# Strided sparse attention and a multiplicative FFN: the first batch's first q and k loads as eight rows a partition with the head pairs stacked on partition halves, and another order of its scores and tails

## The chip, the cores and the metric

The kernel runs on one core of a Trainium2 chip. The metric is the device time of one execution in microseconds (us), here the median of three runs. A profiled execution gives the trace from which the single durations come.

## What is computed

q, k and v have the shape (8 batches, 8 heads, 576 rows, 64), all fp32. Heads 0 to 3 attend to a causal window of 32 keys ("local"), heads 4 to 7 to earlier keys with the same row number modulo 32 ("strided"). The output of the attention, as 4608 tokens of 512, goes through an FFN:

```python
scores = scale * np.matmul(q, k.transpose(0, 1, 3, 2))
scores = np.where(masks[None], scores, -1000000000.0)   # local for h < 4, strided for the others
attn = np.exp(scores - scores.max(-1, keepdims=True))
attn = attn / (attn.sum(-1, keepdims=True) + 1e-09)
x = np.matmul(attn, v)                                  # then (B, H, S, D) -> (B*S, H*D)
out = ((x @ w1) * (x @ w2)) @ w3 @ w_out                # d_model 512, d_ff 1024
```

## The kernel before, in words

Heads are treated in pairs: p0 and p1 are the local pairs of batch 0, p2 and p3 its strided ones. All matmuls take fp16; the inputs are fp32 in HBM and are cast on the chip. q and k must stand with the head dimension on the partitions (two heads of 64 fill 128), so each is loaded with rows on the partitions, cast, transposed by TensorE (a matmul with an identity) into PSUM, and copied to `qT` and `kT`. The first 512 rows of a head go this way with four consecutive rows on a partition (row 4p+c is chunk c of partition p); the last 64 rows, "the rest", are loaded apart (`load_rest`) and transposed in `ah_R`.

The work of the later batches is threaded between the FFN's matmuls of the tokens before. Batch 0 has nothing to hide behind. Its order is written out by hand in `batch0` (L888): `pe` and, while `head[0]` is set, `pin` keep every instruction in program order on its engine. Its parts are:

- `load_first` (L230) issues the q and k loads of batch 0 on SP's queue, group 0 for p0 and p1, group 1 for p2 and p3: 128 partitions, four heads, four rows of 64 floats, so 1 KB pieces. `cast_first` (L239) casts one pair's part with GpSimd ("p"), ScalarE ("a") or VectorE ("v"). SP's queue then holds the rest, group 1, the four loads of v for the local heads (`load_vL`), and the weights. v for the strided heads (`load_vN`, L277) is issued by ScalarE.
- `T1`, that is `ah_T1` (L442), makes one pair's transposes of q (0) or k (1); `ah_T1c` (L455) copies them out, q of the local pairs on ScalarE, k on VectorE.
- `ah_bias` (L538) writes a mask's bias into a score buffer (pool `psB`, two buffers); `sc`, that is `ah_S0`, adds the scores of half of the query groups, and ScalarE takes the exp into the pair's `ptm` or `nptm`. The second half (`sc(p, 1)`) of the local pairs needs the rest rows.
- `ah_tail` copies 16-row tails of a strided pair's exp to `emb`. `ah_PV` multiplies with v and VectorE normalizes; `ph_T2` transposes the output (pool `psM`, one buffer) and copies it to `xT`, the FFN's input. p1's PV needs the second part of `v16L`: a cast (`stage["l"][1][0]`) and then the copy of a 32-row halo (`stage["l"][1][1]`, `halo`).
- `warm` issues small matmuls whose result nobody reads; they take a buffer of pool `psF` (three buffers), which `T1` and `ah_PV` use too.
- `batch0b` begins the FFN's first matmuls (`aps`) with p0's output and the first part of w1, which GpSimd casts as it lands.

From there the FFN's matmuls run to the end, with the attention of the later batches among them.

Of the kernel before, what the change touches and what calls it, by code (L numbers as in the profile page):

```python
# [8 lines left out]
FP32 = mybir.dt.float32  # L9
# [10 lines left out]
def kernel(  # L20
# [11 lines left out]
    nc = tc.nc  # L32
    B, H, S, D = q.shape
# [3 lines left out]
    P = 128  # L37
# [13 lines left out]
    NM = 512  # L51
# [12 lines left out]
    stgp = ctx.enter_context(tc.tile_pool(name="stgp", bufs=9))  # L64
# [10 lines left out]
    def pe(ins):  # L75
        return tc.keep_in_program_order(ins)
# [6 lines left out]
    def half_rows(u):  # L83
        return slice(64 * u, 64 * u + 64)
# [6 lines left out]
    def copy(eng, out, in_):  # L91
        if eng == "a":
            return pin(nc.scalar.copy(out=out, in_=in_))  # L93
        elif eng == "v":
            return pin(nc.vector.tensor_copy(out=out, in_=in_))  # L95
        return pin(nc.gpsimd.tensor_copy(out=out, in_=in_))  # L96
# [3 lines left out]
    id16 = idw[:, 0:P]  # L100
# [108 lines left out]
    x16 = {}  # L209
# [18 lines left out]
    stage = {}  # L228

    def load_first(grp):  # L230
        for nm, ten in (("q", q), ("k", k)):
            st = stgp.tile([P, 4, 4 * D], FP32, tag="stg", name="st")
            t = qkp.tile([P, 2, 4, 2, D], FP16, tag=f"{nm}{grp}", name="t")
            nc.sync.dma_start(st, ten[0, 4 * grp:4 * grp + 4, 0:NM].rearrange("h (p c) d -> p h (c d)", c=4))
            stage[(nm, grp)] = st
            for i in range(2):
                x16[(nm, 2 * grp + i)] = t[:, i]

    def cast_first(nm, hp, eng):  # L239
        h0 = 2 * (hp % 2)  # L240
        st = stage[(nm, hp // 2)]
        return copy(eng, x16[(nm, hp)], st[:, h0:h0 + 2].rearrange("p h (c d) -> p c h d", c=4))
# [73 lines left out]
    for b in range(B):  # L316
        for hp in range(4):
            s = Pair()
# [123 lines left out]
    def ah_T1(s, i, dst=None):  # L442
        if dst is None:
            dst = psF.tile([P, 2 * NM], FP16, tag="f", name="tps")[:, 0:NM]
        if s.b:
            src = x16[(s.b, "qk"[i], s.hp // 2)]
            h0 = 2 * (s.hp % 2)
        else:
            src, h0 = x16[("qk"[i], s.hp)], 0
        for c in range(4):  # L450
            pe(nc.tensor.transpose(dst[:, c * P:(c + 1) * P],  # L451
                                   src[:, c, h0:h0 + 2].rearrange("p h d -> p (h d)"), id16))
        return dst

    def ah_T1c(s, i, dst, eng=None):  # L455
        t = (qT, kT)[i]
        eng = eng or ("v" if i or s.nat and s.b == 0 else "a")
        if s.local:
            copy(eng, t[:, s.hp, 0:NM].rearrange("x (p c) -> x p c", c=4),
                 dst.rearrange("x (c p) -> x p c", c=4))  # L460
        elif i:
            copy(eng, t[:, s.hp, 0:NM], dst)
        else:
            copy(eng, t[:, s.hp].rearrange("x (c w) -> x c w", w=NW)[:, :, 0:P],
                 dst.rearrange("x (c p) -> x c p", c=4))
# [72 lines left out]
    def ah_bias(s, g, wide=True):  # L538
        kr = s.kr
        cs, lo, hi = ah_group(s, g)  # L540
        if wide:
            sps = psB.tile([P, 2, NB], FP32, tag="big", name="sps")
            outs, full = [sps[:, 0], sps[:, 1]], sps
        else:
            outs, full = [psF.tile([P, NB], FP32, tag="f", name="sph") for _ in range(2)], None
        for h in range(2):
            pe(nc.tensor.matmul(outs[h][0:kr, 0:hi - lo], id16[0:kr, 0:kr], s.bias[:, lo:hi], start=True, stop=False))  # L547
        s.sc = getattr(s, "sc", {})
        s.sc[g] = (outs, full)
# [29 lines left out]
    def ah_PV(s, g):  # L579
        cs, lo, hi = ah_group(s, g)  # L580
        ptm, end = ah_home(s)
        if s.b == 0 or s.local:
            xps = psF.tile([P, NB], FP32, tag="f", name="xpl")[:, 0:390].rearrange("p (h x) -> p h x", h=2)
        else:
            xps = psB.tile([P, 2, NB], FP32, tag="big", name="xps")
        for i, c in enumerate(cs):
            for h in range(2):
                c0 = ah_off(s, g) + h * (hi - lo) + s.q[c] - lo
                m = min(P, end - c0)
                o = xps[0:m, h, i * 65:(i + 1) * 65]  # L590
                tail = s.nat and c == NC
                pe(nc.tensor.matmul(o, ptm[0:s.kr, c0:c0 + m],
                                    s.v[0:s.kr, 2 * (s.hp % 2) + h, c, :], start=True, stop=not tail))
                for e in range(NC if tail else 0):
                    e0 = h * 256 + e * 64
                    pe(nc.tensor.matmul(o, emb[:, s.hp - 2, e0:e0 + P], s.v[:, 2 * (s.hp % 2) + h, e, :],
                                        start=False, stop=e == NC - 1))
        if g == 0:
            s.xqs = att.tile([P, LT, 2, D], FP16, tag="xqs", bufs=2, name="xqs")
        norm(s, xps[0:s.kr, :, 0:len(cs) * 65], cs[0], len(cs))  # L600
# [9 lines left out]
    def ph_T2(s, pool=psM, tag="m", n=0):  # L610
        fill = n
        n = s.n
        ps = pool.tile([P, 1024], FP16, tag=tag, name="t2")

        def tr(t, k, o, j=0):
            pe(nc.tensor.transpose(ps[:, o:o + k], s.xqs[0:k, t].rearrange("p h d -> p (h d)"), idw[0:k, j:j + k]))  # L616

        for t in range(n):
            if s.local:
                tr(t, s.q[t + 1] - s.q[t], s.q[t], 0 if t else P - 32)  # L620
            else:
                tr(t, YW if s.nat and t == NC else P, t * P)
        o = xT[s.hp][:, S * s.b:S * s.b + S]
        warm(ps, fill, 384)
        if s.local:
            copy("a", o, ps[:, 0:S])
        elif s.nat:
            copy("a", o[:, 0:NM].rearrange("x (p c) -> x p c", c=4), ps[:, 0:NM].rearrange("x (c p) -> x p c", c=4))
            copy("v", o[:, NM:S], ps[:, NM:S])
        else:  # L630
            ov = o.rearrange("x (t a c) -> x t a c", a=8, c=4)
            nc.scalar.copy(out=ov[:, :, 0:7], in_=ps[:, 0:NM].rearrange("x (c y) -> x y c", c=4)[:, 1:P - 1]
                           .rearrange("x (t a) c -> x t a c", a=7))
            nc.vector.tensor_copy(out=ov[:, :, 7], in_=ps[:, NM + 28:NM + 28 + YW].rearrange("x (t c) -> x t c", c=4))
# [234 lines left out]
    p0, p1, p2, p3 = pairs[0:4]  # L869
# [6 lines left out]
    def both(s):  # L876
        ah_bias(s, 0)
        ah_bias(s, 1)

    def sc(s, g):  # L880
        ah_S0(s, (g,), False)
# [5 lines left out]

    def batch0():  # L888
        head[0] = True
        cast_first("q", 0, "p")  # L890
        cast_first("q", 1, "a")
        both(p0)
        w = psF.tile([P, 1024], FP16, tag="f", name="warm")
        warm(w, 5)
        t = [T1(p0, 0), T1(p1, 0)]
        for s in (p0, p1):
            ah_T1c(s, 0, t[s.hp])
        load_vN(0)
        warm(w, 3)
        cast_first("k", 0, "v")  # L900
        cast_first("k", 1, "p")
        ah_T1c(p0, 1, ah_T1(p0, 1, psM.tile([P, 1024], FP16, tag="m", name="tps")[:, 0:NM]))
        warm(w, 4)
        ah_T1c(p1, 1, T1(p1, 1))
        copy("p", *stage["r"])
        warm(psF.tile([P, 1024], FP16, tag="f", name="warm"), 8)
        sc(p0, 0)
        ah_R(0)()
        sc(p0, 1)
        cast_first("q", 2, "p")  # L910
        cast_first("q", 3, "p")
        cast_first("k", 2, "v")
        cast_first("k", 3, "p")
        ah_bias(p1, 0)
        sc(p1, 0)
        t = [T1(p2, 0)]
        ah_bias(p1, 1)
        ah_T1c(p2, 0, t[0], "a")
        sc(p1, 1)
        ah_T1c(p2, 1, T1(p2, 1))  # L920
        ah_T1c(p3, 0, T1(p3, 0))
        ah_bias(p2, 0)
        stage["l"][0][0]("p")
        stage["l"][0][1]("v")
        sc(p2, 0)
        ah_T1c(p3, 1, T1(p3, 1))
        ah_bias(p2, 1)
        sc(p2, 1)
        stage["x"]("p")
        stage["l"][1][0]("p")  # L930
        ah_PV(p0, 0)
        ah_bias(p3, 0)
        sc(p3, 0)
        ah_tail(p2, 0)
        ah_tail(p2, 1)
        ah_PV(p0, 1)
        ah_bias(p3, 1)
        sc(p3, 1)
        ah_PV(p2, 0)
        ph_T2(p0)  # L940
        ah_PV(p2, 1)
        ah_tail(p3, 0)
        ah_tail(p3, 1)
        stage["l"][1][1]("a")
        ah_PV(p3, 0)
        ah_PV(p3, 1)
        ph_T2(p2)
        ah_PV(p1, 0)
        ah_PV(p1, 1)
        head[0] = False  # L950
# [29 lines left out]
    for p, s in enumerate(pairs):  # L980
        b, i = divmod(p, 4)
# [77 lines left out]
    for jc in range(KF):  # L1059
        h0, h1 = fold_mm(jc)  # L1060
# [95 lines left out]
```

## Time and profile before

| what | value |
|---|---|
| median of three runs | 267.95 us (267.46 to 268.63) |
| profiled execution: time | 267.3 us |
| profiled execution: span on the core | 265.6 us |
| TensorE's granted clock, mean | 0.998 |
| TensorE matmul busy | 259.7 us, 98% of the span |
| VectorE, ScalarE, GpSimd busy | 60%, 53%, 38% |
| HBM traffic over the span | 38.80 MB read, 9.44 MB written |

The profiled execution's time is what the device took; its span goes from the first to the last recorded instruction of the core. In the profile PE is TensorE's matmuls, PEld its weight loads, DVE VectorE, ACT ScalarE, POOL GpSimd and SP the SyncE, whose queue issues most DMAs. A row of the timeline has the start, the length, the engine, the line, the operation, output<-input, shapes and a count; in brackets the idle time before it and what ended it. A row of the chain of waits has start, length and what. A row of the windows has the stretch, its length, the busy time and count of PE, PEld, DVE, ACT and POOL, the granted clock, the mean busy share of the DMA engines and GB/s. Casts and copies that go through the helper `copy` have the lines L93 (ScalarE), L95 (VectorE) and L96 (GpSimd), whatever they copy.

### The profile page before, as it was taken

How to read it: one execution, taken by the hardware profiler on the slowest of the kernel's cores; microseconds unless marked ns; L12 is line 12 of the kernel's file. 1: busy time of each engine (PE TensorE's matmuls, PEld its weight loads, DVE VectorE, ACT ScalarE, POOL GpSimd, SP SyncE). 2: the span in 40 equal slices, each digit the busy share in tenths (PEclk: the TensorE clock that was granted, in tenths of full speed). 3: DMA queues.
4: the chain of work that ended last, by engine and by line, in shares of the span. 5: the costliest groups of instructions: out<-in, count | busy, mean ns of one | idle time of the engine just before them, and what ended most of it. 6: DMA issues, size and time to landing. Idle time of an engine off the chain costs nothing.

```text
span 265.6 us, 6880 instructions
## 1 busy us (share of the span) xinstructions
PE 259.7 (98%) x2730; PEld 137.7 (52%) x2730; DVE 158.1 (60%) x373; ACT 140.1 (53%) x299; POOL 101.3 (38%) x124
## 2 busy tenths in 40 slices
PE   6999999999999999999999999999999999999995
PEld 5664465555555555555555555555555544444442
DVE  7684443655767777867776777577866752421320
ACT  4674342766666655565556565555557634333322
POOL 7687876866239327602730273038200000000000
PEclk9999999999999999999999999999999999999999
DMA  7999999978388588339823973397330022013004
GB/s 224 350 406 407 416 406 311 243 203 261 129 228 237 194 244 224 111 122 269 241 69 124 283 210 119 118 247 225 109 121 2 0 79 82 0 39 121 0 12 147
DMA packets 61100, 48.68 MB, mean 183 GB/s; under 512 B 31804, under 2 KB 52492, under 8 KB 61068
## 3 DMA queue, kind: packets, MB, share of 16 engines
q1 hardware_dynamic: 56236, 40.38, 49.6%
q10 hardware_dynamic: 4832, 7.87, 8.0%
q8 instruction: 21, 0.34, 0.5%
q14 instruction: 11, 0.09, 0.1%
HBM read 38.80 MB, written 9.44 MB: 182 GB/s over the span
## 4 chain that ended last, share of the span: by engine, by line
PE 91%; ACT 3%; DVE 2%; DMA 2%; issue 0%; SPq 0%; ACTq 0%
PE ops L775 29%; PE aps L723 23%; PE bps L732 22%; PE sps L438 3%; PE pt L350 2%; PE t2a L642 2%; PE sps L401 2%; DMA st<-in_k_dram 2%; PE tps L451 1%; PE sps L535 1%; DVE ptm L413 1%; PE t L616 1%; ACT pte L424 1%; PE sps L547 1%; PE trp L833 1%; ACT nptm L560 1%
## 5 line engine op out<-in xcount | busy, mean ns | idle before, releaser
L723 PE MATMUL aps<-xT,w1h 128*128 128x512 f16 (+1 forms) x288 | 73.2, 376 | 0.2
L732 PE MATMUL bps<-xT,w2h 128*128 128x512 f16 (+1 forms) x288 | 73.1, 376 | 0.0
L735 DVE TENSOR_TENSOR abt<-bps,asb 128x512 f16<-128x512 f32 (+1 forms) x72 | 48.6, 679 | 36.8 <-PE bps L732 34.5
L96 POOL CAST t<-st 128x1024 f16<-128x1024 f32 (+1 forms) x49 | 46.3, 955 | 57.4 <-DMA st<-in_q_dram 44.7
L93 ACT COPY asb<-aps 128x512 f32<-128x512 f32 (+1 forms) x71 | 41.3, 584 | 50.7 <-PE aps L723 44.8
L775 PE MATMUL ops<-w,abt 128*128 128x512 f16 x280 | 67.1, 379 | 0.0
L732 PEld LDWEIGHTS <-w2h 128*128 128x128 f16 x288 | 27.1, 98 | 30.9 <-issue 0.7
L723 PEld LDWEIGHTS <-w1h 128*128 128x128 f16 x288 | 26.9, 98 | 28.8 <-issue 0.3
L775 PEld LDWEIGHTS <-abt 128*128 128x128 f16 x280 | 25.2, 98 | 26.2
L424 ACT ACTIVATE pte<-sps 128x1024 f16<-128x1024 f32 (+1 forms) x24 | 24.4, 1018 | 13.2 <-PE sps L401 12.8
L786 ACT COPY osb<-ops 128x512 f32<-128x512 f32 x35 | 21.0, 599 | 19.5 <-PE ops L775 19.5
L607 DVE TENSOR_TENSOR xqs<-sps,rcp 128x768 f16<-128x768 f32 (+1 forms) x24 | 21.4, 891 | 0.8
L413 DVE TENSOR_TENSOR ptm<-pte,maskE 128x1152 f16<-128x1152 f16 (+2 forms) x16 | 12.3, 770 | 7.3 <-ACT pte L424 6.7
L413 DVE TENSOR_TENSOR ptm<-pte,maskX 126x1152 f16<-126x1152 f16 x12 | 11.5, 958 | 7.6 <-ACT pte L424 7.6
L775 PE MATMUL ops<-woh,w3T 128*128 128x512 f16 x64 | 15.3, 380 | 0.0
L95 DVE COPY kT<-pt 128x512 f16<-128x512 f16 (+4 forms) x28 | 11.4, 416 | 6.4 <-ACT kT L93 4.6
L93 ACT COPY qT<-pt 128x224 f16<-128x224 f16 (+4 forms) x40 | 15.0, 424 | 0.2 <-PE pt L358 0.2
L96 POOL CAST v16L<-st 96x768 f16<-96x768 f32 x16 | 13.2, 824 | 4.7 <-DMA st<-in_v_dram 3.7
L309 POOL CAST v16X<-st 126x1024 f16<-126x1024 f32 x6 | 7.4, 1230 | 19.3 <-DMA st<-in_v_dram 15.2
L438 PEld LDWEIGHTS <-ptm 128*128 128x128 f16 (+1 forms) x264 | 11.0, 98 | 6.0 <-DVE ptm L413 1.4
L95 DVE COPY xT<-t2a 128x384 f16<-128x384 f16 (+1 forms) x22 | 8.5, 388 | 7.3 <-PE t2a L642 6.7
L93 ACT COPY kT<-pt 128x224 f16<-128x224 f16 x24 | 8.5, 353 | 6.7 <-DVE qT L95 6.4
(130 smaller groups left out, 286.0 us busy)
## 6 DMA issues: line engine op xcount, KB each, us to landing
st<-in_q_dram SPq DMA_DIRECT2D x16, 512.0 KB
st<-in_k_dram SPq DMA_DIRECT2D x16, 512.0 KB
st<-in_moe_w_dram SPq DMA_DIRECT2D x16, 512.0 KB
out_dram<-osb ACTq DMA_DIRECT2D x27, 256.0 KB
st<-in_v_dram SPq DMA_DIRECT2D x32, 144.0 KB
st<-in_v_dram SPq DMA_DIRECT2D x24, 112.0 KB
st<-in_moe_w_out_dram SPq DMA_DIRECT2D x4, 512.0 KB
out_dram<-osb SPq DMA_DIRECT2D x8, 256.0 KB
```

What stands on the lines that cost most here:

```text
L93: return pin(nc.scalar.copy(out=out, in_=in_))
L95: return pin(nc.vector.tensor_copy(out=out, in_=in_))
L96: return pin(nc.gpsimd.tensor_copy(out=out, in_=in_))
L413: nc.vector.tensor_mul(o.rearrange("p (a x) -> p a x", x=x), i.rearrange("p (a x) -> p a x", x=x), _ap(s.mask, lo, [[s.mask.ap[0][0], s.kr ...
L424: nc.scalar.activation(out=pv[0:kr, :, lo:hi], in_=src, func=AF.Exp, bias=0.0, scale=scale)
L438: pe(nc.tensor.matmul(s.ps[:, h, c * 65:c * 65 + 65], s.ptm[0:s.kr, c0:c0 + P], s.v[0:s.kr, 2 * (s.hp % 2) + h, c, :], start=True, stop=True))
L607: pin(nc.vector.tensor_mul(s.xqs[0:w, c0:c0 + l].rearrange("p i h d -> p h i d"), xv[:, :, :, 0:D], _ap(rcp, 0, [[rcp.ap[0][0], w], [LT, 2 ...
L723: pe(nc.tensor.matmul(st["a"][:, 0:nt], w1h[:, ci, bass.ds(jc * P, P)], xT[ci][:, tok], start=(ci == 0), stop=(ci == last)))
L732: pe(nc.tensor.matmul(st["b"][:, 0:nt], w2h[:, ci, bass.ds(jc * P, P)], xT[ci][:, tok], start=(ci == 0), stop=(ci == KM - 1)))
L735: nc.vector.tensor_mul(abts[tch][:, jc, skip:], st["b"][:, 0:nt], st["asb"][:, 0:nt])
L775: pe(nc.tensor.matmul(st["ps"], lhs(ci), rhs(ci), start=(ci == 0), stop=(ci == KF - 1)))
L786: nc.scalar.copy(out=osb, in_=ps)
```

## The change

Group 0's q and k of batch 0 are each loaded by two DMAs. DMA i fills partitions 64i to 64i+63 with the two heads of pair i, eight consecutive rows a partition (2 KB pieces). `cast_half` casts four of the eight chunks over all 128 partitions, for both pairs at once; both of k's casts go to VectorE (one was GpSimd's). `ah_T1` then makes, for p0 and p1, eight transposes of 64 partitions in place of four of 128, and `ah_T1c` copies them out in order of eight. Other edits: p1's first scores and bias stand between p0's first and second; the second halo copy of v goes from ScalarE to GpSimd, right after its cast; p0's output transposes (`ph_T2(p0)`) stand behind p3's tails and first PV.

```diff
--- before.py
+++ after.py
@@ -229,12 +229,22 @@
 
     def load_first(grp):
         for nm, ten in (("q", q), ("k", k)):
-            st = stgp.tile([P, 4, 4 * D], FP32, tag="stg", name="st")
             t = qkp.tile([P, 2, 4, 2, D], FP16, tag=f"{nm}{grp}", name="t")
-            nc.sync.dma_start(st, ten[0, 4 * grp:4 * grp + 4, 0:NM].rearrange("h (p c) d -> p h (c d)", c=4))
+            if grp == 0:
+                st = stgp.tile([P, 2, 8 * D], FP32, tag="stg", name="st")
+                for i in range(2):
+                    nc.sync.dma_start(st[64 * i:64 * i + 64],
+                                      ten[0, 2 * i:2 * i + 2, 0:NM].rearrange("h (p c) d -> p h (c d)", c=8))
+            else:
+                st = stgp.tile([P, 4, 4 * D], FP32, tag="stg", name="st")
+                nc.sync.dma_start(st, ten[0, 4 * grp:4 * grp + 4, 0:NM].rearrange("h (p c) d -> p h (c d)", c=4))
             stage[(nm, grp)] = st
             for i in range(2):
                 x16[(nm, 2 * grp + i)] = t[:, i]
+
+    def cast_half(nm, i, eng):
+        st = stage[(nm, 0)].rearrange("p h (c d) -> p c h d", c=8)
+        return copy(eng, x16[(nm, i)], st[:, 4 * i:4 * i + 4])
 
     def cast_first(nm, hp, eng):
         h0 = 2 * (hp % 2)
@@ -445,8 +455,14 @@
         if s.b:
             src = x16[(s.b, "qk"[i], s.hp // 2)]
             h0 = 2 * (s.hp % 2)
-        else:
+        elif s.nat:
             src, h0 = x16[("qk"[i], s.hp)], 0
+        else:
+            r = half_rows(s.hp)
+            for c in range(8):
+                pe(nc.tensor.transpose(dst[:, 64 * c:64 * c + 64],
+                                       x16[("qk"[i], c // 4)][r, c % 4].rearrange("p h d -> p (h d)"), id16[r, r]))
+            return dst
         for c in range(4):
             pe(nc.tensor.transpose(dst[:, c * P:(c + 1) * P],
                                    src[:, c, h0:h0 + 2].rearrange("p h d -> p (h d)"), id16))
@@ -456,8 +472,9 @@
         t = (qT, kT)[i]
         eng = eng or ("v" if i or s.nat and s.b == 0 else "a")
         if s.local:
-            copy(eng, t[:, s.hp, 0:NM].rearrange("x (p c) -> x p c", c=4),
-                 dst.rearrange("x (c p) -> x p c", c=4))
+            n = 4 if s.b else 8
+            copy(eng, t[:, s.hp, 0:NM].rearrange("x (p c) -> x p c", c=n),
+                 dst.rearrange("x (c p) -> x p c", c=n))
         elif i:
             copy(eng, t[:, s.hp, 0:NM], dst)
         else:
@@ -887,9 +904,10 @@
 
     def batch0():
         head[0] = True
-        cast_first("q", 0, "p")
-        cast_first("q", 1, "a")
-        both(p0)
+        cast_half("q", 0, "p")
+        cast_half("q", 1, "a")
+        ah_bias(p0, 0)
+        ah_bias(p1, 0)
         w = psF.tile([P, 1024], FP16, tag="f", name="warm")
         warm(w, 5)
         t = [T1(p0, 0), T1(p1, 0)]
@@ -897,8 +915,8 @@
             ah_T1c(s, 0, t[s.hp])
         load_vN(0)
         warm(w, 3)
-        cast_first("k", 0, "v")
-        cast_first("k", 1, "p")
+        cast_half("k", 0, "v")
+        cast_half("k", 1, "v")
         ah_T1c(p0, 1, ah_T1(p0, 1, psM.tile([P, 1024], FP16, tag="m", name="tps")[:, 0:NM]))
         warm(w, 4)
         ah_T1c(p1, 1, T1(p1, 1))
@@ -906,13 +924,13 @@
         warm(psF.tile([P, 1024], FP16, tag="f", name="warm"), 8)
         sc(p0, 0)
         ah_R(0)()
-        sc(p0, 1)
+        sc(p1, 0)
         cast_first("q", 2, "p")
         cast_first("q", 3, "p")
         cast_first("k", 2, "v")
         cast_first("k", 3, "p")
-        ah_bias(p1, 0)
-        sc(p1, 0)
+        ah_bias(p0, 1)
+        sc(p0, 1)
         t = [T1(p2, 0)]
         ah_bias(p1, 1)
         ah_T1c(p2, 0, t[0], "a")
@@ -927,7 +945,8 @@
         ah_bias(p2, 1)
         sc(p2, 1)
         stage["x"]("p")
-        stage["l"][1][0]("p")
+        for f in stage["l"][1]:
+            f("p")
         ah_PV(p0, 0)
         ah_bias(p3, 0)
         sc(p3, 0)
@@ -937,12 +956,11 @@
         ah_bias(p3, 1)
         sc(p3, 1)
         ah_PV(p2, 0)
-        ph_T2(p0)
         ah_PV(p2, 1)
         ah_tail(p3, 0)
         ah_tail(p3, 1)
-        stage["l"][1][1]("a")
         ah_PV(p3, 0)
+        ph_T2(p0)
         ah_PV(p3, 1)
         ph_T2(p2)
         ah_PV(p1, 0)
```

More of the change, by code (lines that the diff above doesn't have):

```diff
@@ L447, in ah_T1 @@
             h0 = 2 * (s.hp % 2)
-        else:
-            src, h0 = x16[("qk"[i], s.hp)], 0
+        elif s.nat:
+            src, h0 = x16[("qk"[i], s.hp)], 0
+        else:
+            r = half_rows(s.hp)
[3 more added lines that the diff above has]
+            return dst
         for c in range(4):
```

## Prediction

> **What bounds the kernel.** I read the page's busy shares first, then the chain of waits over the first 45 us, then the timeline of the first 18 us, then the DMA rates by window. The page says that TensorE is the kernel:
>
> ```profile
> span 265.6 us, 6880 instructions
> PE 259.7 (98%) x2730; PEld 137.7 (52%) x2730; DVE 158.1 (60%) x373; ACT 140.1 (53%) x299; POOL 101.3 (38%) x124
> ```
>
> From 17.43 us on the chain is nearly all matmuls in a fixed order, none of which the diff touches. So the change is worth what it does to the moment at which that stretch starts. The chain up to there (start, length, what):
>
> ```profile
> 1.31 4.81 DMA st<-in_k_dram
> ...
> 6.14 0.44 DVE t L95
> ...
> 6.63 0.40 PE tps L451 x4
> ...
> 7.49 0.45 PE warm L142 x8
> 7.94 0.26 PE sps L535 x8
> 8.20 0.34 PE rps L487 x4
> ...
> 9.82 0.33 PE tps L451 x4
> ...
> 16.13 0.73 ACT v16L L93
> ...
> 16.91 0.53 PE xpl L592 x12
> 17.43 0.86 PE aps L723 x4
> ```
>
> To be seen: k's first load ends the first wait, q does not; the first scores (7.94) stand behind eight warm-up matmuls; and the last wait before the dense stretch is a copy of v's halo on ScalarE, for which p1's PV (16.91) waits. The same stretch by instruction:
>
> ```profile
> 0.80 1.28 ACT L93 ACT_TABLE_LOAD   x1 [0.80 <-PEq L1140]
> ...
> 4.62 0.62 ACT L93 CAST t<-st 128x512 f16<-128x512 f32 x1 [2.53 <-DMA st<-in_q_dram]
> 4.65 0.63 POOL L96 CAST t<-st 128x512 f16<-128x512 f32 x1
> ...
> 5.77 0.59 ACT L93 COPY qT<-tps 128x512 f16<-128x512 f16 x1 [0.54 <-PE tps L451]
> ...
> 6.25 0.59 ACT L93 COPY qT<-tps 128x512 f16<-128x512 f16 x1
> ```
>
> To be seen: the table load is over at 2.08, and ScalarE then idles 2.53 us for q; its cost is hidden. Two windows give the DMA rate (last column), the first while q and k come in 1 KB rows, the second while weights come in 2 KB rows:
>
> ```profile
> 2.30:4.50 2.20, 2.20 (x16) 1.69 (x16) 2.13 (x11) 0.00 (x0) 1.97 (x5) 1.00 0.98 327
> 14.00:22.00 8.00, 7.78 (x96) 4.95 (x96) 5.41 (x19) 5.42 (x13) 6.31 (x8) 1.00 1.05 407
> ```
>
> **Loads.** q's 524 KB take 1.60 us at 327 GB/s and 1.29 at 407, so 2 KB rows would land q 0.31 us earlier (4.31 instead of 4.62) and q with k 0.62 earlier (k at 5.5 instead of 6.12). No row shows a 2 KB load on 64 partitions; the bounds are no gain (4.62, 6.12) and the full gain, and I take the full one, because the weights' rows have the same 2 KB. The Trainium skill, "DMA: Bandwidth & Descriptors", section "Rules for kernel authors", speaks against the split: two transfers to disjoint partition halves serialize, and one of 128 partitions is asked for; by the reading that nothing is gained the sum would be 0.3 us worse (+0.1). Two more issues (0.45 and 0.49 us for the old ones) push every later load on SP's queue, rest, second q and k and the four v loads, about 1 us back. The cover is the backlog: the second q was issued at 3.28 and its first cast ran at 8.44. Without it the second k, cast at 9.90, would come at 10.9 and hold p2's transposes (10.53) by 0.4 us.
>
> **q's casts: the term that speaks against the change.** Each cast now reads all 128 partitions of both q loads, so ScalarE's cast has two loads to wait for. In the changed program ScalarE's list begins: wait for the second q load, table load, cast. The load of 1.28 us, free before, stands behind q. So ScalarE's cast ends at 4.31 + 0.02 + 1.28 + 0.62 = 6.23 (6.54 with q at 4.62) instead of 5.24. GpSimd's is unchanged at 5.28. Every pair's transposes now need both casts, so both pairs wait for 6.23. From cast to first qT copy took 0.49 before (5.28 to 5.77): 6.72. The second copy is 0.48 behind and ends 0.59 later, at 7.79. In the changed program the eight warm matmuls take over the buffer of p1's q transposes and so wait for that copy: 7.79 + 0.02 + 0.45 = **8.26 for the first scores against 7.94**.
>
> **k's casts** both go to VectorE: 5.5 + 0.43 + 0.43 = 6.36, hidden under q's 6.23 plus the remaining twelve q transposes in TensorE's order (0.34 to 0.68 us, from 16 alternating ones of 64 columns in 0.40 and eight of 128 in 0.61), so about 6.8, then three warm matmuls: k's transposes at 7.0, kT copies at 7.4 and 8.0, the second ending at 8.7 (0.69 each before, pitch 0.6). With k at 6.12 all of that still ends before 8.9, so k's gain is worth nothing while q is late. The 0.87 us cast that GpSimd loses is idle time gained. The 32 transposes of 64 columns in place of 16 of 128 lie in this q and k stretch and nowhere else.
>
> **Order of the scores.** Before, p0's second scores waited for the copies of the rest rows (0.26 us of TensorE idle at 8.98), and ScalarE idled 0.28 before its second exp. Now: scores p0 8.26 to 8.52, rest transposes to 8.86, scores p1 to 9.12; exp p0 at 8.56 to 9.26; bias p0 second waits for that end (two score buffers) and runs 9.31 to 9.53, scores to about 9.8, then p2's q transposes at 9.8, where they were before (9.82). The new order gives back the 0.3 us that the table load took. By queueing that I can't resolve (exp p1 ends 9.94 and releases the next bias) I put the exps that follow **+0.1** us, between -0.1 and +0.3; with q at 4.62, +0.3 more.
>
> **Tail.** ScalarE loses the halo copy (16.13 to 16.86), and p3's mask tails no longer stand behind p0's output copy. ScalarE: last exp ends 15.2, tails to 15.67, p0's output copy (0.63) to 16.3; its PSUM buffer frees p2's output transposes (0.26 in the chain): 16.6; p1's PV 0.53: **17.13 instead of 17.43, -0.3**. GpSimd takes the halo: its row for that copy in later batches is 0.81 us (32x640). It sits after the last v cast, which ended at 15.04, so 15.9, ahead of p1's PV at 16.6; the 0.58 us that GpSimd waited for the first w1 swallows most of it, and w1's first cast ends 15.9 + 1.04 = 16.9 instead of 16.66, still before 17.13. The weights' later casts have 1 us and more until their matmuls.
>
> **Sum**: +0.1 - 0.3 = -0.2 us (between -0.4 and +0.3). The profiled execution took 267.3 us, 1.7 over its span, and lies 0.65 below the median of 267.95; the difference is applied to the median: 267.8. A measurement of this kernel can tell about 0.5%, 1.34 us, from no change, so this is "same".
>
> **Rivals.** *The table load has a tail* (slower). Its row ends at 2.08, but nothing ran on ScalarE until 4.62, so anything up to 2.53 us after it would be unseen there and now falls on q's path. Each us of it moves the first scores by one, as no other wait stands behind q by more than 0.5. Price: up to +2.5, so up to 270.3; it passes the bound from 1.5 us of tail on. For it: the cast now follows the load directly, which the trace never shows. Against: the row itself is a whole instruction with an end. Chance 0.18, two thirds of it beyond the bound, since I can't exclude late halves on top. The Trainium skill, "ScalarE: Activation LUTs", section "What ACT_TABLE_LOAD costs", gives about 1283 ns for the load, with which the row of 1.28 us agrees, and about 1380 ns of drain with it, which no row here shows; with that estimate the time would be 269.2.
>
> *The load's wait doesn't bind* (q's second half lands so early, or the load runs before the wait): then k sets the scores: k cast 6.36, kT at 6.9, scores at 7.6, 0.3 earlier, the order's 0.3 is a gain, the tail's 0.3 too: -0.9, 267.1. For it: the load has no data to wait for. Against: it stands behind the wait in the list. Chance 0.14, of which 0.04 beyond the bound.
>
> *GpSimd becomes late*: v's natural load is issued by ScalarE behind the qT copies, at 7.0 instead of 6.14. If it lands 0.9 later (v16X cast at 13.5, not 12.63), GpSimd's row of 1.6 + 0.82 + 0.81 + 1.04 us ends at 17.8, and the first FFN matmul waits for w1 until then: +0.4, 268.4. Against: the v loads ahead of it on SP's queue also move by 1 us. Chance 0.08.
>
> **Numbers.** The forecast has 0.60. Faster is 0.04 (the second rival's far end), slower 0.12 (two thirds of the first), the rest 0.84. The forecast's own range is 267.5 to 268.3. The range goes from a little under the second rival, 266.9, to 269.3, a tail of 1.7 us; some 0.1 lies above it and less below, the spread of the runs before (267.46 to 268.63) counted in.
>
> **What would show it.** Table load right behind q's landing (about 4.3), ScalarE's cast near 5.6, first scores near 8.3; second exp without idle time before it; no halo on ScalarE; first FFN matmul at 17.1 to 17.4. Wrong if the cast starts well after the load's end, if q lands after 4.62, if w1's cast ends after 17.1, or if the dense stretch gets longer by itself.

## The result and the profile after

The changed kernel takes 272.26 us (median of six runs, 271.51 to 273.26); the kernel before took 268.38 (median of six, with the three shown above). The ratio is 1.015, with a 95% interval of 1.0118 to 1.0183; ratios here compare undisturbed runs of both kernels only. So the change costs 4 us, outside the range of the prediction, and on the side that had a chance of 0.12.

The page's busy shares of the profiled execution after (271.51 us):

```profile
span 269.8 us, 6920 instructions
PE 262.7 (97%) x2746; PEld 139.4 (52%) x2746; DVE 159.2 (59%) x374; ACT 139.7 (52%) x298; POOL 100.2 (37%) x124
```

The chain of waits over its first 60 us (start, length, what):

```profile
1.62 3.80 DMA st<-in_q_dram
...
5.49 1.28 ACT L93
...
6.79 0.63 ACT t L93
...
10.13 0.97 PE warm L142 x8
11.10 0.39 PE sps L552 x8
...
15.70 0.23 PE sps L552 x4
...
20.89 0.37 PE xpl L609 x12
21.26 0.86 PE aps L740 x4
```

The dense stretch now starts at 21.26 instead of 17.43, 3.83 us later; that is nearly all of the loss. At the first scores the changed kernel is 3.16 us late (11.10 instead of 7.94), at p2's first scores 4.26 (15.70 instead of 11.44), and 0.4 us of that is made up from there to the dense stretch. The timeline shows what the first scores wait for:

```profile
5.49 1.28 ACT L93 ACT_TABLE_LOAD   x1 [5.49 <-DMA st<-in_q_dram]
5.55 0.61 POOL L96 CAST t<-st 128x512 f16<-128x512 f32 x1 [0.90 <-DMA st<-in_q_dram]
...
6.79 0.62 ACT L93 CAST t<-st 128x512 f16<-128x512 f32 x1
...
7.59 0.76 DVE L95 CAST t<-st 128x512 f16<-128x512 f32 x2 [2.07 <-DMA st<-in_k_dram]
...
10.06 1.04 PE L142 MATMUL warm<-idw 128*128 128x128 f16 x8
...
12.11 0.62 POOL L96 CAST t<-st 128x512 f16<-128x512 f32 x1 [0.87 <-DMA st<-in_k_dram]
```

To be seen: q lands at 5.5 (it was forecast at 4.3, and was 4.6 before), k at 7.6 (forecast 5.5, before 6.1); the table load does stand behind q; eight warm matmuls take 1.04 us where they took 0.61; and the second group's k, untouched by the change, is cast at 12.11 instead of 9.93 (L96). The windows over the loads (last column GB/s) show that q and k came at a lower rate than before, not a higher one (258 against 327 between 2.30 and 4.50 us, 205 against 348 in the half microsecond behind it):

```profile
2.30:4.50 2.20, 2.20 (x16) 1.70 (x16) 2.13 (x11) 0.00 (x0) 1.97 (x5) 1.00 0.91 258
4.50:5.00 0.50, 0.50 (x3) 0.30 (x2) 0.50 (x4) 0.00 (x0) 0.14 (x1) 1.00 0.81 205
```

### The profile page after: what moved, and what is told of

Read it like the earlier page. It is cut to its first block, busy times and chain, and to the rows that moved or that the text cites. A ratio compares the mean times of both kernels' runs of the same rounds, so it can differ in the third digit from the quotient of the medians.

```text
span 269.8 us, 6920 instructions
## 1 busy us (share of the span) xinstructions
PE 262.7 (97%) x2746; PEld 139.4 (52%) x2746; DVE 159.2 (59%) x374; ACT 139.7 (52%) x298; POOL 100.2 (37%) x124
## 3 DMA queue, kind: packets, MB, share of 16 engines
q10 hardware_dynamic: 4832, 7.87, 7.9%
## 4 chain that ended last, share of the span: by engine, by line
PE 92%; ACT 3%; DMA 1%; DVE 1%; issue 0%; SPq 0%; ACTq 0%
PE ops L792 28%; PE aps L740 22%; PE bps L749 22%; PE sps L448 3%; PE t2a L659 2%; PE sps L411 2%; PE pt L360 2%; DMA st<-in_q_dram 1%; PE tps L467 1%; PE sps L552 1%; PE t L633 1%; DVE ptm L423 1%; PE sps L564 1%; ACT pte L434 1%; PE warm L142 1%; PE trp L850 1%
## 5 line engine op out<-in xcount | busy, mean ns | idle before, releaser
L96 POOL CAST t<-st 128x1024 f16<-128x1024 f32 (+1 forms) x48 | 46.8, 982 | 62.6 <-DMA st<-in_q_dram 37.0
L96 POOL CAST v16L<-st 96x768 f16<-96x768 f32 x16 | 13.2, 827 | 7.1 <-DMA st<-in_v_dram 5.3
L319 POOL CAST v16X<-st 126x1024 f16<-126x1024 f32 x6 | 6.3, 1049 | 16.6 <-DMA st<-in_v_dram 16.6
```

## The experiments

Four theories of where the 4 us come from were tried: the load into half the partitions is slow; the two extra issues on SP's queue make everything behind them late; the table load behind q is on the path; TensorE runs at half pitch. Rivals stand with each.

The diffs of this section are shortened; `...` and the remarks behind `#` stand for what is left out.

**The load change alone**: the changed kernel (its loads, casts and transposes) with the order of scores and the tails of before.

```diff
-        ah_bias(p0, 0); ah_bias(p1, 0)        # and sc(p0,0), sc(p1,0), sc(p0,1), sc(p1,1)
+        both(p0)                              # and sc(p0,0), sc(p0,1), sc(p1,0), sc(p1,1)
-        for f in stage["l"][1]: f("p")        # ph_T2(p0) behind ah_PV(p3, 0)
+        stage["l"][1][0]("p")                 # [1]("a") ahead of ah_PV(p3, 0), ph_T2(p0) ahead of ah_PV(p2, 1)
```

> The change's load, casts and transposes alone, with the order of scores and the tails of the kernel before. Theory 'the load is the whole loss': 272 to 273 us, as the changed kernel or up to 0.6 us above it (the prediction's gain from order and tail). Rival 'the order shares the loss': nearer to before, 270 us or less.

273.15 us, ratio 1.0186 (1.0143 to 1.0229). The load, with its casts and transposes, is the whole loss. First FFN matmul at 22.50, later than in the changed kernel (21.10).

**The order and the tails alone**: the opposite half, on the kernel before.

```diff
-        both(p0)
+        ah_bias(p0, 0)
+        ah_bias(p1, 0)
...
-        stage["l"][1][0]("p")
+        for f in stage["l"][1]:
+            f("p")
...
```

> The kernel before with the change's order of scores and its tails alone, its loads and casts as before. By the prediction's terms: 0.3 us from the order of the scores and 0.3 us from the tail, first FFN matmul at about 16.9 instead of 17.4, 267.5 to 268.0 us. Rival 'the order itself costs': first FFN matmul at 17.4 or later and a time at or above that of before.

269.32 us, ratio 1.0005 (0.9963 to 1.0048): no difference that can be told. The gain of 0.6 us (0.2%) that the prediction had for these edits lies inside the interval, as does no gain. Its profiled execution took 272.31 us, 3 us above that median, so no stretch of it is read.

**The DMA rates by themselves**: eight stretches of loads ahead of the kernel before.

```diff
+    section((full,), lambda i: rows(q, i, 2, 4), 2)           # 128 partitions, 1 KB rows
+    section((lo,), lambda i: rows(k, i, 2, 8), 2)             # 0 to 63, 2 KB
+    section((mid,), lambda i: rows(q, i, 2, 8), 2)            # 32 to 95, 2 KB
+    section((lo, hi), lambda i: rows(k, i, 2, 8), 2)          # both halves in turn, 2 KB
+    section((lo, hi), lambda i: rows(q, i, 2, 8), 2, two_queues=True)
+    section((lo,), lambda i: rows(k, i, 4, 4)[0:64], 4)       # 0 to 63, 1 KB
+    section((mid,), lambda i: rows(q, i, 4, 4)[0:64], 4)      # 32 to 95, 1 KB
+    section((full,), lambda i: moe_w3[...], 2, n=8)           # 128 partitions, weights
```

> The kernel before with a prologue of eight stretches of loads, 256 KB each (512 KB in the last), into xT's later home; only the DMA rate of each stretch is of interest. Stretches: 1 KB rows on 128 partitions; 2 KB rows on partitions 0 to 63; 2 KB rows on 32 to 95; 2 KB rows on 0 to 63 and 64 to 127 in turn; the same on two queues; 1 KB rows on 0 to 63; 1 KB rows on 32 to 95; weights, 128 partitions, 2 KB. Theory 'half the partitions, half the write paths' (64 partitions in one half of the 128 reach fewer of them): about 220 GB/s for 0 to 63 with either row length, 350 to 400 for 32 to 95, 128 partitions as in the kernel before (370 and 410). Rival 'it is the 2 KB rows of q and k as they lie in HBM': low with 2 KB on any partitions, 350 with 1 KB. Rival 'it is 64 partitions as such': low on 32 to 95 too.

One window inside each stretch, in that order (GB/s last):

```profile
4.00:12.00 8.00, 1.70 (x11) 1.08 (x9) 1.52 (x6) 0.00 (x0) 0.64 (x1) 1.00 1.03 343
18.00:32.00 14.00, 0.00 (x0) 0.00 (x0) 0.00 (x0) 0.00 (x0) 0.00 (x0) 1.00 1.07 211
36.00:44.00 8.00, 0.00 (x0) 0.00 (x0) 0.00 (x0) 0.00 (x0) 0.00 (x0) 1.00 1.05 386
48.00:60.00 12.00, 0.00 (x0) 0.00 (x0) 0.00 (x0) 0.00 (x0) 0.00 (x0) 1.00 1.06 254
66.00:78.00 12.00, 0.00 (x0) 0.00 (x0) 0.00 (x0) 1.28 (x1) 0.00 (x0) 1.00 1.04 232
84.00:98.00 14.00, 0.00 (x0) 0.00 (x0) 0.00 (x0) 0.00 (x0) 0.00 (x0) 1.00 1.12 210
103.00:111.00 8.00, 0.00 (x0) 0.00 (x0) 0.00 (x0) 0.00 (x0) 0.00 (x0) 1.00 1.09 383
114.00:122.00 8.00, 0.00 (x0) 0.00 (x0) 0.00 (x0) 0.00 (x0) 0.00 (x0) 1.00 1.03 421
```

This settles that a load into one half of the partitions is slow, the first theory; what it costs the kernel is another question. Partitions 0 to 63 take 211 GB/s with 2 KB rows and 210 with 1 KB; the same number of partitions from 32 to 95 takes 386 and 383. So it is neither the row length nor 64 partitions as such, but which 64. (Nor is it the tensor: q is read at 386 in one stretch and at 232 in another.) The first window has the slow start of the loads in it; from 10 to 12 us the 128 partitions with 1 KB rows take 384, no more than the 64 from 32 to 95. The changed kernel loads 0 to 63 and then 64 to 127: that pattern takes 254, and 232 when the halves go on two queues. The Trainium skill, "SBUF — State Buffer", section "Door 1: The DMA port swizzle (why `[64,N]` ≈ `[32,N]`)", says that the rate depends on how many of 16 ports the partitions reach, and that the ports are split between the lower and the upper 64 partitions. The rows agree: 211 is 0.55 of 386. The rows show besides that two halves hardly overlap even on two queues (232).

**The cut into halves in the kernel before**: its own 1 KB rows, casts and order.

```diff
-            nc.sync.dma_start(st, src)
+            for part in (slice(0, 64), slice(64, P)):
+                nc.sync.dma_start(st[part], src[part])     # group 0 only
```

> The kernel before with its first q and k loads cut into two DMAs of 64 partitions each (four heads, 1 KB rows as before); casts, order and all else as before. Theory 'half the partitions are slow': q lands near 5.4 instead of 4.6 and k near 7.5 instead of 6.1, and as k ends the first wait, the first scores come 1.4 us later: about 270 us. Rival 'the 2 KB rows are slow': q and k within 0.3 us of before, and the time at 268.5.

272.22 us, ratio 1.0147 (1.0079 to 1.0216): the changed kernel's time, without its rows, stacking, casts or order, and 2 us more than the theory gave. The run adds two issues on SP's queue too, so it doesn't tell half the partitions from more issues; the next one does. q's cast on GpSimd is at 6.05, k's on VectorE at 8.05. ScalarE's cast waits for two loads here too, so the table load stands behind q, at 5.99.

**The cut by heads**: as many DMAs, but each on all 128 partitions.

```diff
-            nc.sync.dma_start(st, src)
+            for part in (slice(0, 2), slice(2, 4)):
+                nc.sync.dma_start(st[:, part], src[:, part])   # group 0 only
```

> The kernel before with its first q and k loads cut into two DMAs of two heads each on all 128 partitions; same number of DMAs as in the changed kernel, same 1 KB rows as before. Theory 'half the partitions are slow': no change, q at 4.6 to 4.8, k at 6.1 to 6.3, time 268.5. Rival 'two more issues cost': q near 5.4, k near 7.5, about 270 us.

271.9 us, ratio 1.0106 (1.0062 to 1.0149). The time is nearer to the rival's, but by another way than the rival gave: neither theory had this. The profiled execution is one of the quicker ones (269.62 us, 2.3 above the profiled one of before). q and k land as early as before or earlier (ScalarE's cast at 4.28, VectorE's at 5.81), and still it is slow. VectorE's rows show the place:

```profile
5.81 0.43 DVE L95 CAST t<-st 128x512 f16<-128x512 f32 x1 [0.29 <-DMA st<-in_k_dram]
...
11.38 0.43 DVE L95 CAST t<-st 128x512 f16<-128x512 f32 x1 [1.54 <-DMA st<-in_k_dram]
```

The second group's k comes at 11.38, 1.5 us later than before, GpSimd's first v cast at 13.37 instead of 11.03, its first w1 cast at 17.24 instead of 15.62, and the first FFN matmul at 19.25 instead of 17.27. What is late is what stands behind the two extra issues.

**Two tiny loads**: q and k untouched, two issues more on SP's queue.

```diff
     load_first(0)
+    for i in range(2):
+        nc.sync.dma_start(tiny[:, i], moe_w3[0:P, 8 * i:8 * i + 8])
     load_rest(0)
```

> The kernel before with two loads of 4 KB each put between k and the rest rows on SP's queue: two more issues, q and k themselves untouched. Theory 'the later loads have no cover': the second q and k, v and w1 are each cast 1 us or more later than before (second k's cast after 10.9 instead of 9.90, first w1 cast after 16.6 instead of 15.62), the time is 1 to 2.5 us above before (269.5 to 271). Rival 'the backlog covers it' (the prediction's step): second k's cast at 9.9 to 10.2 and the time at 268.5. If so, what slowed the kernel with two loads by heads was the cut of q and k itself.

270.19 us, ratio 1.0068 (1.0044 to 1.0092). The rows come as the theory has them. SP's row, VectorE's cast of the second k and GpSimd's first cast of w1, from three timelines of this kernel:

```profile
1.84 0.98 SPq L1025 DMA_DIRECT2D tiny<-in_moe_w_dram  x2
```

```profile
10.96 0.43 DVE L95 CAST t<-st 128x512 f16<-128x512 f32 x1 [1.17 <-DMA st<-in_k_dram]
```

```profile
18.22 1.04 POOL L96 CAST w1h<-st 128x1024 f16<-128x1024 f32 x1 [1.05 <-DMA st<-in_moe_w_dram]
```

With 0.98 us of issue put in, the second k came at 10.96 instead of 9.90 and w1 at 18.22 instead of 15.62. Between 6 and 7 us this kernel moved 173 GB/s where the kernel before moved 366; but the mean busy share of the DMA engines was 1.20 there (1.14 before), so they were slow rather than without work.

And this kernel has a second difference, which the run was not made to have. Its loads are slower from end to end. The page gives the time of all packets of SP's queue (packets, MB, share of 16 engines' span), before and here:

```profile
q1 hardware_dynamic: 56236, 40.38, 49.6%
```

```profile
q1 hardware_dynamic: 56524, 40.39, 56.0%
```

Between 22 and 30 us, where only weights come, it moved 388 GB/s, the kernel before 408. The two kernels with `early` below have the same (56.2 and 56.9%, 388 GB/s); the nine others with the bytes of before, changed or not, have 48.3 to 50.1% and 405 to 408. What sets the three apart is that each adds a small tile on the chip, `tiny` or `early`. Whether that moves the places where the loads land, and so slows them, no run here tests. So the 1.8 us of this run are not the price of two issues alone; for that the cut by heads (49.6%) is the better witness.

**The table load at the start.**

```diff
+    pe(nc.vector.memset(early, 0.0))
+    pe(nc.scalar.copy(out=early[:, 0:4], in_=early[:, 4:8]))
     make_identity(nc, id16)
```

> The changed kernel with one tiny ScalarE copy at the very start, so that the table load runs at once. Theory 'the table load is on the path': ScalarE's cast starts with q's landing (5.5) instead of 6.79, TensorE's 0.85 us of idle time before 7.46 is gone, the first scores and the end come 1.3 us earlier (about 271.0 us). Rival 'k's landing hides it': k lands at 7.59 in the changed kernel and its transposes start at 8.44 right behind its casts, so the first scores move by less than 0.3 us and the time stays at 272.3. By the theory of the clock there is a third way: less idle time lets TensorE reach its fast pitch (56 instead of 121 ns a warm matmul) earlier than 15.2 us, and the gain is 2 us or more.

273.35 us, ratio 1.0161 (1.0103 to 1.0219): no gain. The time can't decide, as this kernel's loads are slow from end to end. Its rows speak for the rival: ScalarE's cast comes at 5.45, and k's landing takes its place:

```profile
5.45 0.62 ACT L93 CAST t<-st 128x512 f16<-128x512 f32 x1 [3.15 <-DMA st<-in_q_dram]
...
7.72 0.76 DVE L95 CAST t<-st 128x512 f16<-128x512 f32 x2 [2.21 <-DMA st<-in_k_dram]
...
8.21 0.62 PE L466 MATMUL tps<-idw,t 64*128 64x64 f16 x8 [1.24 <-DVE t L95]
...
9.84 1.04 PE L145 MATMUL warm<-idw 128*128 128x128 f16 x8
10.81 0.45 PE L555 MATMUL sps<-qT,kT 64*128 64x96 f16 x8
```

First scores at 10.81 instead of 11.03. The changed kernel's own rows say the same: k's second cast ends at 8.35 there, and k's transposes start at 8.44. The profile also shows what the 1.04 us of eight warm matmuls are: its windows have TensorE's granted clock (third column from the end) at half there:

```profile
9.00:12.00 3.00, 3.00 (x40) 2.15 (x37) 1.41 (x4) 0.70 (x1) 1.78 (x3) 0.50 1.17 312
12.00:15.00 3.00, 3.00 (x34) 1.83 (x28) 1.14 (x6) 2.42 (x5) 1.23 (x2) 0.50 1.19 264
```

In the changed kernel's profile the column reads 1.00 at the same place, with the same 1.04 us for the same eight matmuls; the pitch, not the column, tells the clock in the first microseconds of an execution.

**TensorE kept busy**: more warm matmuls in the waits for q's casts.

```diff
-        warm(w, 5)
+        warm(w, 11)
+        hook[0] = lambda: warm(w, 14)     # run between the fourth and the fifth transpose of p0's q
```

> The changed kernel with 20 more warm matmuls in TensorE's waits for the casts of q (6 before the first transposes, 14 between the fourth and the fifth), so that it never idles between 5 and 7.5 us. Theory 'slow clock': warm matmuls at 56 ns from about 8.5 us on instead of about 15.2, scores and transposes up to the second group at full pitch, 1.5 to 2.5 us less (about 270 us). Rival 'the slow stretch is chance, not idle time': pitch stays at 121 ns until about 15, and the time is that of the changed kernel, 272.3, or worse by what the 20 matmuls take.

271.08 us, ratio 1.0096 (1.0057 to 1.0134), 1.2 us below the changed kernel, with intervals that just overlap (1.0118 is the lower end of the changed kernel's). In the profiled execution the pitch is full in time, 0.62 us for the eight, and the first scores come 1.0 us earlier:

```profile
9.46 0.62 PE L143 MATMUL warm<-idw 128*128 128x128 f16 x8
10.01 0.33 PE L556 MATMUL sps<-qT,kT 64*128 64x96 f16 x8
```

The first FFN matmul then waits for w1: 20.43 instead of 21.10.

**Fewer warm matmuls in the kernel before**: 3 instead of 20 ahead of the first transposes.

```diff
-    warm(..., 6); warm(..., 9); warm(w, 5)
+    warm(..., 1); warm(..., 1); warm(w, 1)
```

> The kernel before with 3 warm matmuls instead of 20 ahead of its first transposes, so that TensorE reaches its fast pitch later; loads, casts and order as before. Theory 'slow clock': the first scores come at nearly the same place (k's landing) but the stretch from there to the first FFN matmul runs at 121 ns a transpose instead of 56 until the clock opens, 1 to 2.5 us more: 269.5 to 271 us. Rival 'the pitch of TensorE does not matter while other engines are waited for': within 0.5 us of before.

269.06 us, ratio 1.0022 (0.9987 to 1.0057). First scores at 8.82 instead of 7.87 and first FFN matmul at 18.43 instead of 17.27 in its profile, but the times can't be told from before. So where the loads are in time a late clock costs 1.2 us in the profile and at most 1.5 us (the interval's upper end) in the times; expected were 1 to 2.5.

**Second halves on ScalarE's queue.**

```diff
-                    nc.sync.dma_start(st[64 * i:64 * i + 64],
+                    (nc.sync, nc.scalar)[i].dma_start(st[64 * i:64 * i + 64],
```

> The changed kernel with the second half of each load (partitions 64 to 127) issued on ScalarE's queue, so that both halves are in flight at once. Theory 'a load into half the partitions is slow by itself': q lands at 4.6 to 4.9 instead of 5.44 and k at 6.1 to 6.5 instead of 7.55, about 1 us less at the end (271.2). Rival 'two more issues are what delays it': SP issues two fewer, so q and k come 0.6 to 1.2 us earlier too, but the DMA rate while q alone is in flight stays at 260 to 330 GB/s; if the rows of 2 KB are slow, nothing moves.

271.35 us, ratio 1.0109 (1.0079 to 1.014). q (5.47) and k (7.63) land no earlier, which speaks against both of the theories as far as q and k go: SP's issues don't hold them, and two halves in flight are no faster than one after the other (the stretch on two queues, 232 GB/s, says the same). What comes earlier is what SP issues behind them, the second k at 11.04 instead of 12.11. The median is 0.9 us below the changed kernel's, but the intervals overlap (1.0118 to 1.0183 there), so that gain is not secured.

**Three repairs at once**: table load at the start, two queues, filled waits.

> The changed kernel with three repairs at once: table load at the start, the second halves issued on ScalarE's queue (so SP issues no more than before), and the warm matmuls that keep TensorE busy. What is left is the slow load into half the partitions: q at 5.4, k near 7.6, 1.4 us later than before, so 1 to 1.5 us above the kernel before (269.5 to 270). Rival 'there is another cost': 271 us or more. Rival 'the repairs cover the load too': at 268.5.

273.34 us, ratio 1.0194 (1.0169 to 1.0218): the rival of another cost holds, with no gain over the changed kernel. It shares the slow loads of the two kernels with an added tile (56.9%): q lands at 5.9, k at 8.3, v's natural load is cast at 18.0 and w1 at 21.45, and the DMA rate falls to 169 GB/s between 7 and 8 us. TensorE's pitch is full at the eight warm matmuls (0.62 us), but while it waits for v its clock falls back: 0.50 in the column from 19 to 22 us. How much the three repairs would give without the slow loads is not known.

## Why the prediction was wrong

The forecast was 0.2 us less; 4 us more came.

**The loads: the sign was wrong.** The prediction took q 0.31 us earlier and k 0.62 earlier, from the rate of 2 KB rows of weights, and bounded that below by "no gain". q came 0.9 us later, k 1.5. The row length was the wrong likeness: 64 partitions of one half take 210 GB/s with 1 KB or 2 KB. The trace before had a hint: its rate fell to 287 between 5.5 and 6 us, while the rest rows came, which are loaded on 64 partitions each (but in pieces of 256 bytes, so that the row alone could not tell the two apart). The step that failed is the bound: it went from full gain to no gain and left out a loss. The rule that the prediction cites for it (two halves serialize) had the direction, but was priced at nothing gained, 0.3 us.

**The cover of the backlog: wrong, and the issues were longer.** Two more issues were to push the later loads back by about 1 us, and this was to be hidden by the queue of data, with 0.4 us as the price if not. SP's rows after, and the second q's issue before:

```profile
0.80 1.42 SPq L236 DMA_DIRECT2D st<-in_q_dram  x2
2.26 1.26 SPq L236 DMA_DIRECT2D st<-in_k_dram  x2
4.89 0.62 SPq L240 DMA_DIRECT2D st<-in_q_dram  x1
```

```profile
3.28 0.62 SPq L234 DMA_DIRECT2D st<-in_q_dram  x1
```

The four issues took 2.68 us, where the two before took 0.94, so the second q was issued 1.6 us later, not 1. And nothing hid it: the second k was cast 2.2 us later (12.11), v's natural load 2.2 (14.87). The cut by heads shows the step without halves: issues 1.0 us later, the second k 1.5, v 2.3, w1 1.6, the first FFN matmul 2.0, and 1.06% in the time. The 5 us between an issue and a cast were taken for slack, and they were not. The price was asked of p2's transposes alone, not of v and w1.

**The table load: right in place and length, wrong in weight.** It stands behind q, takes 1.28 us, and the cast starts 0.02 us after it: the rival with a tail is false, and of the drain that the prediction cites beside it nothing is seen in that gap. But k, forecast to be hidden, lands so late (7.59) that the load is hidden behind it.

**TensorE's clock: not in the prediction.** Every pitch was taken from the trace before. In the changed kernel the transposes, warm matmuls and first scores ran at half of it until about 15 us: from ScalarE's cast (7.41) to the first scores 3.7 us, where the forecast had 2.0. From k's landing to the first scores it was 3.4 us (7.59 to 11.03), before 1.7 (6.14 to 7.87), and 2.3 in the profile with filled waits (7.75 to 10.01). So of the 3.2 us at the first scores 1.5 are k's later landing and some 1.2 the pitch. At the end filling the waits gave back 1.2 us by the medians; as the intervals overlap and the clock also changes from execution to execution, this share stays rough.

**Order and tails: nothing measurable.** From p2's first scores to the first FFN matmul the chain took 5.6 us after and 6.0 before, the size that was forecast for the tail (0.3); alone on the kernel before the edits give 1.0005. The load without them is 1.0186, with them 1.015.

**GpSimd late**: v's cast did come late (14.87 instead of 12.63), but w1's first cast still ended ahead of the first FFN matmul, so that rival did not decide.

In sum: that the cut load is the whole loss is shown (1.0186 without the other edits, 1.0147 with nothing but the cut into halves). How it divides is not. The cut by heads, with as many issues and no halves, already costs 1.0106, and its interval overlaps that of the cut by halves, so what the slow halves add to the issues can't be told from these times. The parts need not add up to one sum, since each delays other members of the same queue of loads.

## What to carry to other kernels

Half the bytes in partitions 0 to 63 are no half of a load into 128: at 210 GB/s against 384 they take nine tenths of the time of the whole, and both halves in turn (254 GB/s, with 2 KB rows) take half as long again as the whole. Where the head of a kernel is fed by one queue, count each issue as time for everything behind it, down to the weights, and don't take the time that a load has been under way for slack. When an experiment adds a tile, compare the rate of loads that it should not touch. And an operand whose cast waits for two loads can drag one-time work, such as a table load, behind the data.

## What was not expected of the hardware

- 64 partitions take 386 GB/s on 32 to 95 and 211 on 0 to 63; both halves on two queues together take 232. With 1 KB rows 64 partitions from 32 to 95 (383) are as fast as 128 (384).
- TensorE's clock may open at about 5 us and fall back: in one execution it was half from 9 to 15 us. Eight warm matmuls took 0.61 us or 1.04 us by it, and the granted-clock column can read 1.00 in the first microseconds while the pitch is half.
- Three kernels that each add one small tile have slower loads from end to end (388 GB/s instead of 405 to 408 for the weights between 22 and 30 us, 56% instead of 48 to 50% of the engines' span for the same bytes). The cause is not shown.
- Two more issues on SP's queue, with q and k no later, moved v's first cast by 2.3 us and the first FFN matmul by 2.0 in the profiled execution (the cut by heads).
